# Twelve wholes of the first q product in the lead instead of eleven, so that later q products begin and end with a turn

## The chip, the cores and the metric

The kernel runs on one core of one Trainium2 chip. The metric is the device time of one execution in microseconds (us); the median of three runs is given, and one more execution was profiled. Engines are named as in the profile: PE (matrix multiplies, with PEld its weight loads), DVE (vector), ACT (activations), POOL (general), SP (issues most DMAs).

## The reference

```python
h = _layernorm(x) * (1 + ca) + sa
x = x + ga * A(h)          # attention: H = 32 heads of 16, one shared k and v
h = _layernorm(x) * (1 + cb) + sb
x = x + gb * B(h)          # (h @ w_gate) * (h @ w_up) @ w_down
# A: q = h @ wq; k = h @ wk; v = h @ wv
#    p = softmax(q k^T / 4) over all 2048 keys; o = p v; o @ wo
# S = 2048 rows, D = 512, F = 1792; six modulation rows from silu(c) @ w_mod
```

## The kernel before

The 2048 rows are cut into 4 blocks of 512 queries. A *unit* `u` is 4 heads of one block, so there are 32 units, and each runs over 16 key tiles of 128 keys. One key tile of one unit is a *turn*; `attend(u, kt)` writes out two turns. In a turn PE makes four score matmuls (`sc`, L621, `qk_exp`), ACT takes the exponential of each (`P`, L623), and PE multiplies the exponentials of the turn before with v (`pv`, L632, eight instructions into one held bank). Beside that runs a pass that finds the row maxima of a later unit: four matmuls (`mx`, L570) per turn, each reduced by DVE (`mpart`, L574).

Score and max matmuls contract over 50 and 48 rows, so two of them fit in the array at once, in the upper and the lower 64 rows. Projections are fed into the same stream as `Group`s. A q product (`q_proj`, one 128-column part of one query block) is a `Group` of 12 steps. In attention each step is cut into two halves of 64 rows (`half(r)`, L492), which stand in the halves of the array that scores and maxima leave free; before attention a step is one full matmul (`whole()`, L501). All steps of a group add up in one PSUM bank named `side` (L485). There are 16 q products of which the first is not in the queue `qs`; the queue holds 15.

The order inside a turn is written out by hand. While a q product is under way it is

```python
FEW = "e1 m0 e0 x1 m0 x1 e0 x1 m0 x1 e1 m0"    # e score, m max, x half of a product
```

and the odd turn of a pair swaps the halves 0 and 1. So a turn has four places `x` for one half of the array, a pair has eight, and a q product fills three pairs. If a product ends at a place, `side_half` begins the next one in the queue at the following place of the same turn. When no product is left, the order is `NO_SIDE`, without `x`. Later, in the feed-forward stage, it is `MANY`.

When a product has all its halves, it is put in `ended`; after the twelve places of the turn `finish` is called: ACT copies the bank to SBUF (`qf`, L514), POOL splits the copy into two 16-bit parts (L515, L516), SP stores them to DRAM (L518), from where `load_q` (L535) reads them for the max pass of a later unit.

The eight PSUM banks go round in a queue. `ps_mx` and `ps_sc` take the oldest bank and put it at the queue's end at once, so that the next matmul that is given that bank waits for its reader (DVE for `mx`, ACT for `sc`). `ps_hold` takes the oldest bank out of the queue until `ps_give`. During attention one bank is held for `pv`, one for `side`, and one for a short time by the transposition of the maxima (`mxt`, L598, once per unit) and by the sums of the late weights (L916). After the last key tile of a unit ACT copies the `pv` bank out (`ev`, L638).

The first half of a product in a turn also waits for an exponential of the turn before when the product changes its half of the array (L496). A product that begins does not change.

Before attention there are 30 steps of a *lead* (`for n in range(LEAD)`, L1103), which does the first maxima and other preparation. In its last four steps it also emits wholes of `qs[0]`, as many as `Q_BURSTS` says. What is left of `qs[0]` goes to attention.

Of the kernel before, what the change touches and what calls it, by code (L numbers as in the profile page):

```python
# [35 lines left out]
NHF = 12  # L36
M_STEP = 23
PAIRED = 14
Q_BURSTS = {26: 3, 27: 3, 28: 3, 29: 2}

CHANNEL = {0: KC - 1, 3: 0, 4: 1, 6: 2}
LOW = -3.0e38
# [12 lines left out]
def adaln_mqa_glu_kernel(ctx: ExitStack, tc: tile.TileContext, x_in, wq_in, wk_in, wv_in, wo_in,  # L55
# [1047 lines left out]
    for n in range(LEAD):  # L1103
# [6 lines left out]
        if n in first:  # L1110
            first[n]()
        for _ in range(Q_BURSTS.get(n, 0)):
            qs[0].whole()
# [166 lines left out]
```

## Time and profile before

| | |
|---|---|
| median of 3 runs | 1682.76 us (1682.55 to 1683.22) |
| profiled execution | 1682.67 us, of which the span of the program is 1680.6 us |
| PE busy | 1656.3 us, 99% of the span |
| DVE busy | 1390.0 us, 83% |
| ACT busy | 1216.1 us, 72% |
| POOL busy | 518.1 us, 31% |

The busy share of PE alone says little, because matmuls are pipelined and their ends are modelled. What a turn costs is read from the timeline: the distance from a turn's first score matmul (L621) to that of the next. Attention begins at 74.38 us. Turns are counted from 0 below; turn 2 begins at 79.58 us. The q products are in turns 0 to 85.

### The profile page before, as it was taken

The numbers are of one execution on the slowest core, as the hardware profiler recorded it, in microseconds if no ns is written. First come the engines' busy times: TensorE is split into PE (matmuls) and PEld (weight loads), VectorE is DVE, ScalarE is ACT, GpSimd is POOL, SyncE is SP. The second block draws the span as 40 slices with busy tenths as digits, with TensorE's granted clock in tenths as the row PEclk, the third lists the DMA queues.
The fourth block names the chain that finished last, engine by engine and source line by source line (L and its number), as shares of the span: only waits on it lengthen the run. The fifth ranks groups of instructions, "written<-read, shape, count | busy, mean of one in ns | idle before, by whom it ended". The sixth has DMA issues, their size and how long they took to land.

```text
span 1680.6 us, 33352 instructions
## 1 busy us (share of the span) xinstructions
PE 1656.3 (99%) x12749; PEld 535.4 (32%) x12749; DVE 1390.0 (83%) x2365; ACT 1216.1 (72%) x2288; POOL 518.1 (31%) x690
## 2 busy tenths in 40 slices
PE   8999999999999999999999999999999999999999
PEld 3333333222223333333333333333333333334444
DVE  7999999999989999999989999999998999703110
ACT  5688888888787778777777777877777777772010
POOL 5745354626676740200140211101032111112230
PEclk9999999999999999999999999999999999999999
DMA  6112122211321200001100000000010000001000
GB/s 245 72 40 88 54 88 61 94 48 50 84 66 56 85 22 9 17 10 29 35 15 12 15 15 10 16 10 17 24 32 12 23 16 6 12 5 49 13 1 25
DMA packets 48556, 66.33 MB, mean 39 GB/s; under 512 B 14726, under 2 KB 29194, under 8 KB 48396
## 3 DMA queue, kind: packets, MB, share of 16 engines
q1 hardware_dynamic: 46812, 63.87, 12.2%
q8 instruction: 100, 1.64, 0.4%
q14 instruction: 60, 0.49, 0.1%
q10 hardware_dynamic: 1584, 0.33, 0.1%
HBM read 51.05 MB, written 8.65 MB: 36 GB/s over the span
## 4 chain that ended last, share of the span: by engine, by line
PE 87%; DVE 9%; ACT 2%; DMA 1%; issue 0%; ACTq 0%; DVEq 0%
PE side L485 50%; PE pv L632 27%; DVE mpart L574 8%; PE sc L621 5%; PE mx L570 3%; ACT P L623 2%; PE mx L765 1%; DMA xbig<-in_A_x_dram 1%; PE mxt L598 0%; DVE bs L238 0%; PE sc L570 0%; PE pk L274 0%; DMA wkv<-in_A_wv_dram 0%; DVE rel L579 0%; PE part L267 0%
## 5 line engine op out<-in xcount | busy, mean ns | idle before, releaser
L574 DVE TENSOR_REDUCE mpart<-mx 128x1 f32<-128x512 f32 x2016 | 1266.1, 683 | 91.6 <-PE mx L570 88.3
L623 ACT ACTIVATE P<-sc 128x512 f32<-128x512 f32 x2048 | 1092.0, 599 | 264.6 <-PE sc L621 223.1
L621 PE MATMUL sc<-sst,kst 50*128 50x512 f16 x2048 | 661.0, 379 | 1.0 <-DVE mpart L574 0.8
L570 PE MATMUL mx<-kst,sst 48*128 48x512 f16 x2032 | 617.3, 377 | 6.5 <-DVE mpart L574 3.8
L632 PE MATMUL pv<-P,vst 128*32 128x512 f32 x4096 | 545.3, 605 | 1.2
L485 PE MATMUL side<-h2T,wg 64*128 64x512 f16 (+1 forms) x1168 | 284.3, 378 | 0.1
L485 PE MATMUL side<-h2T,wu 64*128 64x512 f16 (+1 forms) x1166 | 282.9, 378 | 0.1
L485 PE MATMUL side<-wd,glu 64*128 64x512 f16 (+1 forms) x1008 | 234.1, 378 | 0.0
L818 POOL TENSOR_SCALAR glu<-gf 128x512 f16<-128x512 f32 x56 | 34.7, 620 | 617.2 <-DVE gf L817 538.9
L621 PEld LDWEIGHTS <-kst 50*128 50x128 f16 x2048 | 175.2, 94 | 129.4 <-issue 109.6
L570 PEld LDWEIGHTS <-sst 48*128 48x128 f16 x2064 | 183.9, 94 | 58.7 <-issue 37.4
L485 PEld LDWEIGHTS <-wg 64*128 64x128 f16 (+1 forms) x1168 | 100.9, 94 | 202.7 <-ACT P L623 95.0
L485 PEld LDWEIGHTS <-wu 64*128 64x128 f16 (+1 forms) x1166 | 100.8, 95 | 200.2 <-ACT P L623 92.5
L632 PEld LDWEIGHTS pv<-P,vst 128*32 128x32 f32 x4096 | 80.8, 108 | 218.8 <-issue 202.8
L485 PEld LDWEIGHTS <-glu 64*128 64x128 f16 (+1 forms) x1008 | 89.1, 95 | 163.2 <-ACT P L623 63.0
L817 DVE TENSOR_TENSOR gf<-side,g 128x512 f32<-128x512 f32 x56 | 38.3, 684 | 115.8 <-PE side L485 82.5
L485 PE MATMUL side<-h,wq 64*128 64x512 f16 (+1 forms) x349 | 92.5, 376 | 0.0
L812 ACT ACTIVATE g<-side 128x512 f32<-128x512 f32 x56 | 33.2, 593 | 81.5 <-PE side L485 81.5
L485 PE MATMUL side<-wo,och 64*128 64x512 f16 (+1 forms) x336 | 79.3, 378 | 0.0
L819 POOL TENSOR_TENSOR glu<-gf,glu 128x512 f16<-128x512 f32 x56 | 65.0, 1161 | 4.7
L200 POOL TENSOR_SCALAR rv<-st 128x1 f32<-128x1 f32 (+1 forms) x20 | 4.6, 228 | 158.3 <-DVE st L725 143.2
L666 POOL TENSOR_TENSOR oc<-oc,rr 128x512 f32<-128x512 f32 x15 | 19.1, 1275 | 107.4 <-DMA sst<-qd 94.3
(223 smaller groups left out, 810.5 us busy)
## 6 DMA issues: line engine op xcount, KB each, us to landing
wsl<-in_B_w_gate_dram SPq DMA_DIRECT2D x32, 224.0 KB
wsl<-in_B_w_up_dram SPq DMA_DIRECT2D x32, 224.0 KB
wsl<-in_B_w_down_dram SPq DMA_DIRECT2D x28, 256.0 KB
sst<-qd SPq DMA_DIRECT2D x180, 32.0 KB
oc<-ev SPq DMA_DIRECT2D x128, 32.0 KB
rr<-ri SPq DMA_DIRECT2D x16, 256.0 KB
xl<-in_A_x_dram SPq DMA_DIRECT2D x16, 256.0 KB
qd<-q SPq DMA_DIRECT2D x15, 256.0 KB
```

The lines of the kernel that those rows point to most:

```text
L485: return nc.tensor.matmul(self.p, left[64 * r0:64 * r1], right[64 * r0:64 * r1], start=start, stop=self.ended())
L570: nc.tensor.matmul(m, s[64 * a:64 * a + 48, p, t * 128:(t + 1) * 128], w[64 * a:64 * a + 48, :], start=(i == 0), stop=(i == len(keys) - 1))
L574: nc.vector.tensor_reduce(part, m, axis=AX.X, op=OP.max)
L621: nc.tensor.matmul(t, kst[64 * a:64 * a + 50, kt * 128:(kt + 1) * 128], s[64 * a:64 * a + 50, p, :], start=True, stop=True)
L623: ex = nc.scalar.activation(ptl[u, kt, p, a], t, AF.Exp)
L632: nc.tensor.matmul(pvb[u][32 * j:32 * j + 32, :], vst[:, kt, :], ptl[u, kt, p, a], start=(kt == 0), stop=(kt == KT - 1))
L666: eng.tensor_tensor(o, o, st["r"], op=OP.mult)
L765: nc.tensor.transpose(st["p"][:, t * 128:(t + 1) * 128], n2s[b, t][:, k * 128:(k + 1) * 128], ident)
L812: nc.scalar.activation(st["g", f], p, AF.Copy, scale=2.0 ** -45)
L817: nc.vector.tensor_tensor(gf, p, st["g", f], op=OP.mult)
L818: nc.gpsimd.tensor_scalar(st["glu"][:, 0, f, :], gf, 1.0, 0.0, op0=OP.mult, op1=OP.add)
L819: nc.gpsimd.tensor_tensor(st["glu"][:, 1, f, :], gf, st["glu"][:, 0, f, :], op=OP.subtract)
```

## The change

The lead emits three wholes of `qs[0]` in its last step instead of two, so that all twelve steps of that product are done, and its `finish`, before attention begins.

```diff
-Q_BURSTS = {26: 3, 27: 3, 28: 3, 29: 2}
+Q_BURSTS = {26: 3, 27: 3, 28: 3, 29: 3}
```

Before, one whole (two halves) of `qs[0]` was left: its first half took one place of turn 0, the other three places of that turn stayed empty, its last half took the first place of turn 1, and the next product took the three places behind it. From there each product began with three halves in an odd turn and ended with one half six turns later. Thirteen turns (7, 13, ..., 79) held the end of one product and the beginning of the next. Now the next product begins at the first place of turn 0, and each one fills six turns: it ends with the last place of turns 5, 11, 17, ..., and the next opens turns 6, 12, 18, ..., 78. The last product ends in turn 83 instead of 85, so turns 84 and 85 are written in the order without places for products. The PE's order and waits from turn 87 on are the same in both kernels.

The order on ACT from the last step of the lead (`modT` is part of the lead's preparation) to the end of the first unit, before:

```order
L195 ACTIVATE modT_177<-mx 128x4x32
L623 ACTIVATE P<-sc 128x512 x8
L514 ACTIVATE qf<-side,qvs 128x512
L623 ACTIVATE P<-sc 128x512 x24
L514 ACTIVATE qf<-side,qvs 128x512
L623 ACTIVATE P<-sc 128x512 x24
L514 ACTIVATE qf<-side,qvs 128x512
L603 ACTIVATE mt_1555<-mxt 16x128
L623 ACTIVATE P<-sc 128x512 x16
L638 ACTIVATE ev<-pv,evs 128x512
L623 ACTIVATE P<-sc 128x512 x8
L514 ACTIVATE qf<-side,qvs 128x512
```

And the same stretch of ACT now:

```order
L195 ACTIVATE modT_177<-mx 128x4x32
L514 ACTIVATE qf<-side,qvs 128x512
L623 ACTIVATE P<-sc 128x512 x24
L514 ACTIVATE qf<-side,qvs 128x512
L623 ACTIVATE P<-sc 128x512 x24
L514 ACTIVATE qf<-side,qvs 128x512
L623 ACTIVATE P<-sc 128x512 x8
L603 ACTIVATE mt_1559<-mxt 16x128
L623 ACTIVATE P<-sc 128x512 x16
L514 ACTIVATE qf<-side,qvs 128x512
L638 ACTIVATE ev<-pv,evs 128x512
L623 ACTIVATE P<-sc 128x512 x24
```

Every copy `qf` stands two turns (eight exponentials) earlier, the first of them ahead of attention; one of them now stands right ahead of the copy `ev` of a unit's end, as another does at the end of the fourth unit, while before the two met once, at the end of the third.

The second half of turn 7 on PE before, where `side_1273` is the bank of the product that begins in this turn (its first half stands just ahead of these rows), `mx_1270` took its bank ahead of them, and the bracket names the engine whose work a matmul waits for:

```order
L621 LDWEIGHTS kst_130
L621 MATMUL sc_1276<-sst0_126,kst_130 128x512 [waits DVE_49]
L485 LDWEIGHTS wq_110
L485 MATMUL side_1273<-h16_178,wq_110 128x512
L570 LDWEIGHTS sst1_127
L570 MATMUL mx_1280<-kst_130,sst1_127 128x512 [waits Activation_49]
L485 LDWEIGHTS wq_110
L485 MATMUL side_1273<-h16_178,wq_110 128x512
L621 LDWEIGHTS kst_130
L621 MATMUL sc_1285<-sst0_126,kst_130 128x512 [waits DVE_49]
L570 LDWEIGHTS sst1_127
L570 MATMUL mx_1288<-kst_130,sst1_127 128x512 [waits Activation_49]
```

The second half of turn 6 on PE now, the first turn that a product opens after another has ended, with `side_1242` its bank:

```order
L621 LDWEIGHTS kst_130
L621 MATMUL sc_1249<-sst0_126,kst_130 128x512 [waits DVE_49]
L485 LDWEIGHTS wq_110
L485 MATMUL side_1242<-h16_178,wq_110 128x512
L570 LDWEIGHTS sst1_127
L570 MATMUL mx_1253<-kst_130,sst1_127 128x512 [waits Activation_49]
L485 LDWEIGHTS wq_110
L485 MATMUL side_1242<-h16_178,wq_110 128x512
L621 LDWEIGHTS kst_130
L621 MATMUL sc_1258<-sst0_126,kst_130 128x512 [waits Activation_49]
L570 LDWEIGHTS sst1_127
L570 MATMUL mx_1261<-kst_130,sst1_127 128x512 [waits DVE_49]
```

Before, two product banks were out of the queue in the second half of such a turn, so the last two max matmuls were given banks that exponentials of the same turn were still to read. Now the ended product's bank is back in the queue before the next product takes one: the third max matmul is given that bank and waits for `qf`, and the last one waits for a DVE reduction, as in a turn within a product.

## The prediction

> **What bounds the kernel now.** I read the page first, then the busy time by windows for the stretch in which the q products run, then the timeline of single turns. Columns of the first row: engine, busy us, instructions; of the window row: length, then busy us (and count) of PE, PEld, DVE, ACT, POOL, the granted clock, DMA share and GB/s; of the timeline: start, duration, engine, line, what.
>
> ```profile
> PE 1656.3 (99%) x12749; PEld 535.4 (32%) x12749; DVE 1390.0 (83%) x2365; ACT 1216.1 (72%) x2288; POOL 518.1 (31%) x690
> 150.00:200.00 50.00, 49.92 (x414) 16.04 (x414) 48.49 (x84) 42.05 (x82) 22.46 (x23) 1.00 0.19 60
> ```
>
> In this stage PE and DVE are both nearly full, ACT has about a sixth of its time free, and the clock is full. Neither PE nor DVE is the limit by itself; a ring of the two is. Turn 6 (89.6 to 92.1) shows it; it lies within a product (first max matmul and its reduction, third and fourth max, `pv`, and the first score of turn 7, which comes together with its first max):
>
> ```profile
> 89.60 0.39 PE L570 MATMUL mx<-kst,sst 48*128 48x512 f16 x1
> 90.05 0.69 DVE L574 TENSOR_REDUCE mpart<-mx 128x1 f32<-128x512 f32 x1
> 90.48 0.38 PE L570 MATMUL mx<-kst,sst 48*128 48x512 f16 x1
> 90.80 0.37 PE L570 MATMUL mx<-kst,sst 48*128 48x512 f16 x1
> 91.10 1.06 PE L632 MATMUL pv<-P,vst 128*32 128x512 f32 x8
> 92.10 0.39 PE L621 MATMUL sc<-sst,kst 50*128 50x512 f16 x1
> ```
>
> The first max matmul starts at 89.60, its reduction runs from 90.05 to 90.74, the fourth max matmul, which is given the same bank, starts at 90.80, `pv` follows 0.30 later, and the next turn 1.00 after that: 2.50 us. Now turn 7, in which one product ends and the next begins (third and fourth max, `pv`, and the first scores of turns 8 and 9, with the ACT and DVE rows between):
>
> ```profile
> 92.52 2.06 ACT L623 ACTIVATE P<-sc 128x512 f32<-128x512 f32 x4 [0.44 <-PE mx L570]
> 93.17 0.37 PE L570 MATMUL mx<-kst,sst 48*128 48x512 f16 x1
> 93.66 0.37 PE L570 MATMUL mx<-kst,sst 48*128 48x512 f16 x1
> 93.96 1.06 PE L632 MATMUL pv<-P,vst 128*32 128x512 f32 x8
> 94.45 0.71 ACT L514 ACTIVATE qf<-side,qvs 128x512 f32<-128x512 f32 x1
> 94.96 0.39 PE L621 MATMUL sc<-sst,kst 50*128 50x512 f16 x1
> 95.41 3.19 DVE L574 TENSOR_REDUCE mpart<-mx 128x1 f32<-128x512 f32 x5 [0.38 <-PE mx L570]
> 97.46 0.39 PE L621 MATMUL sc<-sst,kst 50*128 50x512 f16 x1
> ```
>
> It takes 94.96 - 92.10 = 2.86 us. Four exponentials in 2.06 us, the last one about 0.6, have a pitch of about 0.49, so the first ends at 93.12 and the second at 93.61: exactly 0.05 ahead of the third max matmul (93.17) and the fourth (93.66), which wait for them, since with a second product bank held they were given banks of this turn's scores. DVE then stands still for 0.38 us. So such a turn costs 2.86 - 2.50 = 0.36 us, on the path that sets the pace, and turn 8 (2.50) gives none of it back. That the second bank does it and not the end of a product is shown by turn 85, which has a product's end and no beginning, and takes 299.31 - 296.81 = 2.50:
>
> ```profile
> 294.31 0.39 PE L621 MATMUL sc<-sst,kst 50*128 50x512 f16 x1
> 296.81 0.39 PE L621 MATMUL sc<-sst,kst 50*128 50x512 f16 x1
> 299.31 0.39 PE L621 MATMUL sc<-sst,kst 50*128 50x512 f16 x2
> 304.08 0.39 PE L621 MATMUL sc<-sst,kst 50*128 50x512 f16 x2
> 306.46 0.39 PE L621 MATMUL sc<-sst,kst 50*128 50x512 f16 x2
> ```
>
> **The change, part by part.** *Removed: thirteen mixed turns.* Turns 7, 13, ..., 79 no longer hold two product banks: 13 x 0.36 = 4.68 us less. I take the price of turn 7 for all; those with the weights' sums may give a little more.
>
> *Shorter: turns 84 and 85.* They lose their product places. With such places a turn took 2.50 (294.31 to 296.81), without them 306.46 - 304.08 = 2.38: 2 x 0.12 = 0.24 less.
>
> *Added: the copy `qf` ahead of the exponentials of an opening turn.* It is the same copy as before, but it no longer has the 0.36 of the mixed turn to hide in. Queued behind it on ACT are the four exponentials of the opening turn, for whose first the fourth score matmul waits, and behind that the fourth max. The nearest row is the copy `ev`, equally long, ahead of the exponentials of turn 18, in a turn without a mixed one ahead of it:
>
> ```profile
> 119.12 0.39 PE L621 MATMUL sc<-sst,kst 50*128 50x512 f16 x1
> 121.47 0.71 ACT L638 ACTIVATE ev<-pv,evs 128x512 f32<-128x512 f32 x1
> 121.68 0.39 PE L621 MATMUL sc<-sst,kst 50*128 50x512 f16 x1
> 124.18 0.39 PE L621 MATMUL sc<-sst,kst 50*128 50x512 f16 x1
> ```
>
> Turn 18 takes 124.18 - 121.68 = 2.50: the copy fits in the 0.44 that ACT idles in a plain turn (the row at 92.52), and costs nothing. The third max matmul is to wait for `qf` itself; it would start 2.35 after the start of the turn ahead (as 94.45 - 92.10), end at 3.07, which is 0.57 in the opening turn, and that matmul comes at about 0.88 in a turn (90.48 - 89.60). So I take 0 for the nine opening turns that have nothing else on ACT (6, 12, 24, 36, 42, 48, 54, 60, 72). Bounds: no gain is possible, since the ring from the first max to the fourth stays; at most the whole 0.71 delays ACT instead of the 0.57 after which the next instruction starts in the rows below, 0.14 each, 1.3 in all.
>
> The Trainium skill ("ScalarE: Activation LUTs", section "What ACT_TABLE_LOAD costs") speaks against this a little: by it a copy of 512 columns with one pointer operand takes 186 + 93 + 0.833 x 512 = 706 ns and back-to-back activations overlap by 93 ns, so `qf` would hold ACT for 0.61 us. By that figure each of the nine turns would cost about 0.04, and the gain would be 0.4 us smaller. The trace's 0.71 agrees with the duration; for the overlap it shows more, 0.71 - 0.57 = 0.14.
>
> *Moved: two openings meet a unit's end.* `qf` and `ev` now stand together ahead of turns 18 and 66; before, they met once, ahead of turn 50:
>
> ```profile
> 204.91 0.71 ACT L514 ACTIVATE qf<-side,qvs 128x512 f32<-128x512 f32 x1
> 205.48 0.72 ACT L638 ACTIVATE ev<-pv,evs 128x512 f32<-128x512 f32 x1
> 205.42 0.39 PE L621 MATMUL sc<-sst,kst 50*128 50x512 f16 x1
> 206.05 2.10 ACT L623 ACTIVATE P<-sc 128x512 f32<-128x512 f32 x4
> 206.74 0.37 PE L621 MATMUL sc<-sst,kst 50*128 50x512 f16 x1
> 208.06 0.39 PE L621 MATMUL sc<-sst,kst 50*128 50x512 f16 x1
> ```
>
> Each copy holds ACT 0.57 (204.91 to 205.48 to 206.05). The exponentials start 0.63 in the turn, the fourth score matmul waits for the first of them until 1.32, and the turn ends 1.32 later: 2.64. Now the turn ahead is not 2.86 but 2.56 (turn 17: 121.68 - 119.12, in which `pv` waits for a new bank), so the exponentials start at 2.35 + 0.57 + 0.57 - 2.56 = 0.93, the first ends near 1.57, the score starts at 1.63, and the turn takes 1.63 + 1.32 = 2.95 instead of 2.50. Two such: +0.90. Turn 50 falls to 2.50 (-0.14), and turn 49 keeps 0.06 of `pv`'s wait (+0.06). Bounds for each meeting: 0.14, as in turn 50, and 0.57, a whole copy.
>
> *Moved: two openings meet the transposition of the maxima*, turns 30 and 78. Where `qf` and that step met before:
>
> ```profile
> 235.89 0.71 ACT L514 ACTIVATE qf<-side,qvs 128x512 f32<-128x512 f32 x1
> 236.40 0.28 PE L598 MATMUL mxt<-ident,mm 128*16 128x128 f32 x1
> 236.71 0.27 ACT L603 ACTIVATE mt<-mxt 16x128 f16<-16x128 f32 x1
> ```
>
> There `qf` began 0.51 ahead of the turn and `mt` started at 0.31. Now `qf` begins 0.15 ahead of it (2.50 - 2.35), `mt` starts at 0.57 - 0.15 = 0.42, and DVE's part of it with the reductions behind it 0.11 later: 2 x 0.11 = 0.22 more, between nothing and 0.36 each, all the cover that the mixed turn gave.
>
> *Moved: the twelfth whole and the first `qf` into the lead.* DVE has work there without a gap from 71.51 to 95.04:
>
> ```profile
> 71.51 23.53 DVE L574 TENSOR_REDUCE mpart<-mx 128x1 f32<-128x512 f32 x38 [0.39 <-PE mx L570]
> 72.49 0.82 PE L485 MATMUL side<-h,wq 128*128 128x512 f16 x3
> 73.85 0.60 PE L485 MATMUL side<-h,wq 128*128 128x512 f16 x2
> 74.81 4.18 ACT L623 ACTIVATE P<-sc 128x512 f32<-128x512 f32 x8 [0.63 <-PE mx L570]
> ```
>
> So the third whole (0.82 - 0.60 = 0.22) and the exponentials, which now begin behind `qf`, about 0.5 after 74.81, are covered as long as the eight max matmuls of turns 0 and 1 arrive in time; following their banks by hand, I estimate that each has about 0.3 or more to spare. Without this cover it costs up to 0.5. With it, turn 2 can begin up to 0.1 earlier, since turn 1 was mixed too; I take -0.10. POOL's and SP's shares of `qf` move forward with it; POOL is 31% busy, and they stay behind no work that PE waits for.
>
> *Sum:* -4.68 - 0.24 + 0.90 - 0.14 + 0.06 + 0.22 - 0.10 = -3.98, against the profiled execution's 1682.67 us: 1678.7. That execution lies 0.09 below the median, so the same holds for that. From turn 87 on the program is unchanged and each part starts on other parts' ends or counted turns, so the whole is kept to the end.
>
> **The rivals.** (1) *Openings pay in part.* The exponentials come late in each opening turn: the 1.3 of the bound, 2 x (0.57 - 0.45) = 0.24 more at the meetings, 2 x (0.36 - 0.11) = 0.50 at the transpositions. Gain 3.98 - 2.04 = 1.9, time 1680.7. For it: `qf` is now in a turn without spare time; against it: turn 18. (2) *The time is given back later.* If late weights or their POOL work set the start of the feed-forward stage, the 4 us become a wait there: 1682.7. Against it: POOL's longest waits are for DVE, in the feed-forward stage itself (total us, times, longest), so POOL has time to spare there:
>
> ```profile
> POOL glu L818 <- DVE gf L817: 538.9, 53, 29.2
> ```
>
> (3) *Slower: each opening turn becomes like a meeting.* If the exponentials of all thirteen opening turns begin at 0.93 instead of 0.43, each turn takes 0.45 more: 13 x 0.45 = 5.85, against 4.68 + 0.24 + 0.08 + 0.10 = 5.10 that goes: +0.75, 1683.4. It decides from 5.10 / 13 = 0.39 per opening, for which ACT would have to be held by `qf` about 1.1 us; the `ev` rows show 0.57. (4) *The mixed turn's cost stays*, because it comes from the end of a product and not from the second bank: then nothing goes but 0.24, and the meetings cost 0.9: 1683.4 too. Turn 85 speaks against it.
>
> **How the numbers follow.** Forecast 0.70, rival 1 0.12, rival 2 0.08, rivals 3 and 4 0.06 together, more than 4.8 gained 0.04. The predicted time is that of the forecast, 1678.7. The bounds of its own terms, taken the good way (meetings 0.14 each, transpositions nothing), give 4.8, or 1677.8; some more in the mixed turns with sums gives 1677.5. Upwards the range takes in rival 1 and a part of what lies behind it: 1681.0. About 0.2%, or 3.4 us, is what a measurement of this kernel can tell from no change. The forecast lies 0.6 beyond it, and its dear bounds inside; of its 0.70 I give 0.65 to faster by more than that, with 0.03 of the good tail: 0.68. Rivals 1 and 2 and most of 3 and 4 are within: 0.28. Slower by more: 0.04.
>
> **What would show it.** Right: turns 7, 19, 25 and so on take 2.50; turns 6, 24, 36 take 2.50 with `qf` ahead of their exponentials; DVE has no idle of 0.38 at a product's beginning; turns 18 and 66 take about 2.95; turn 86 begins about 4.0 earlier than before, and the end as well. Wrong: opening turns of 2.6 or more everywhere (rival 1 or 3), a later wait of PE that grew by what was saved (rival 2), or the last two max matmuls of some turn in six still waiting for exponentials (rival 4).

## The result, and the profile after

The changed kernel takes 1679.41 us (median of 14 runs), the kernel before 1683.27 us beside it: a ratio of 0.9978, 95% interval 0.9971 to 0.9985. The forecast was 1678.7 us, faster by more than can be told from no change. The profiled execution takes 1679.23 us, 3.44 less than that of before; its span is 1677.1. A turn is counted from its first score matmul to that of the next.

The page's engine row and the window that was shown of before (length, then busy us and count of PE, PEld, DVE, ACT, POOL, granted clock, DMA share, GB/s), now of the changed kernel:

```profile
PE 1652.6 (99%) x12748; PEld 535.7 (32%) x12748; DVE 1389.8 (83%) x2365; ACT 1214.6 (72%) x2288; POOL 518.0 (31%) x690
150.00:200.00 50.00, 49.57 (x418) 16.12 (x415) 49.08 (x86) 42.55 (x84) 24.45 (x26) 1.00 0.19 56
```

DVE is busier in the same 50 us (49.08 instead of 48.49) because it no longer stands still once in six turns; PE is 0.35 less busy, which is a new wait, shown below. The timeline of the changed kernel around turns 6 and 7 (the first score of turns 6, 7 and 8, third and fourth max of turn 6, the ACT rows of turns 5 and 6, and DVE):

```profile
87.55 2.06 ACT L623 ACTIVATE P<-sc 128x512 f32<-128x512 f32 x4 [0.44 <-PE mx L570]
88.79 8.79 DVE L574 TENSOR_REDUCE mpart<-mx 128x1 f32<-128x512 f32 x14
89.47 0.71 ACT L514 ACTIVATE qf<-side,qvs 128x512 f32<-128x512 f32 x1
89.63 0.39 PE L621 MATMUL sc<-sst,kst 50*128 50x512 f16 x1
90.05 2.09 ACT L623 ACTIVATE P<-sc 128x512 f32<-128x512 f32 x4
90.52 0.38 PE L570 MATMUL mx<-kst,sst 48*128 48x512 f16 x1
90.83 0.37 PE L570 MATMUL mx<-kst,sst 48*128 48x512 f16 x1
92.13 0.39 PE L621 MATMUL sc<-sst,kst 50*128 50x512 f16 x1
94.63 0.39 PE L621 MATMUL sc<-sst,kst 50*128 50x512 f16 x1
```

Turn 7 takes 94.63 - 92.13 = 2.50 instead of 2.86. Turn 6, which a product now opens, takes 2.50 as well: `qf` sits in ACT's idle time, the exponentials start 0.42 in the turn, the third max comes at 0.89 with `qf`'s bank free by then, and the fourth at 1.20. DVE's fourteen reductions run without a gap. Where an opening meets a unit's end it is otherwise (turns 17 and 18; the fourth score of turn 18 is the row at 122.56):

```profile
118.38 0.39 PE L621 MATMUL sc<-sst,kst 50*128 50x512 f16 x1
120.73 0.71 ACT L514 ACTIVATE qf<-side,qvs 128x512 f32<-128x512 f32 x1
121.30 0.72 ACT L638 ACTIVATE ev<-pv,evs 128x512 f32<-128x512 f32 x1
120.94 0.39 PE L621 MATMUL sc<-sst,kst 50*128 50x512 f16 x1
121.87 2.10 ACT L623 ACTIVATE P<-sc 128x512 f32<-128x512 f32 x4
122.56 0.37 PE L621 MATMUL sc<-sst,kst 50*128 50x512 f16 x1
123.88 0.39 PE L621 MATMUL sc<-sst,kst 50*128 50x512 f16 x1
```

The exponentials start 0.93 in the turn, the fourth score at 1.62, and the turn takes 2.94 instead of 2.50. Turn 66 takes the same. And one turn became slower that the prediction expected to become shorter, turn 31. Its rows, with those of turn 30 that lead to it (PE's `mxt` stands ahead of the first score of turn 30; the scores at 154.34 and 157.34 open turns 31 and 32):

```profile
151.41 0.28 PE L598 MATMUL mxt<-ident,mm 128*16 128x128 f32 x1
152.11 0.28 DVE L604 SCALAR_TENSOR_TENSOR mt<-mxt,mt 16x128 f16<-16x128 f32 x1
152.76 1.16 POOL L516 TENSOR_TENSOR q<-qf,q 128x512 f16<-128x512 f32 x1
153.95 0.33 SPq L518 DMA_DIRECT2D qd<-q  x1
154.32 0.42 SPq L897 DMA_DIRECT2D wsl<-in_B_w_gate_dram  x1
154.84 1.23 SPq L608 DMA_DIRECT2D sst<-mt  x2
154.34 0.39 PE L621 MATMUL sc<-sst,kst 50*128 50x512 f16 x1
157.34 0.37 PE L621 MATMUL sc<-sst,kst 50*128 50x512 f16 x1 [0.43 <-DMA sst<-mt]
```

Before, the two DMAs that bring the maxima to the next unit's scores were issued 0.61 after that `mxt` (152.42):

```profile
153.03 1.22 SPq L608 DMA_DIRECT2D sst<-mt  x2
```

Now they are issued 3.43 after it (154.84 - 151.41), although `mt` is ready at 152.39 (152.11 + 0.28): on SP they stand behind the product's store `qd`, which waits until 153.92 for POOL's second split (152.76 + 1.16), and behind a weight load. The first score of the next unit waits for them, and turn 31 takes 3.00.

The distance between the first scores of turns 2 and 87 holds all places of q products but those of turns 0 and 1. It is free of the lead, which ends at other times in other executions (turn 2 begins between 78.95 and 80.93 us in the profiles of this study), and so it is compared below, in us. Each ratio is to runs of the kernel before that were made beside that kernel (medians 1683.27, 1683.03 and 1683.00).

| kernel | turn 2 to turn 87 | median of all runs | ratio to before, 95% interval |
|---|---|---|---|
| before | 222.13 | 1683.27 | |
| changed | 218.55 | 1679.41 | 0.9978 (0.9971 to 0.9985) |
| no begin where another ends | 218.82 | 1679.20 | 0.9978 (0.9969 to 0.9987) |
| store half a turn later | 218.08 | 1678.88 | 0.9976 (0.9967 to 0.9985) |
| lead alone | 222.35 | 1683.30 | 1.0001 (0.9992 to 1.0010) |
| further bank held | 223.08 | 1684.51 | 1.0006 (0.9997 to 1.0015) |
| changed, again | 218.51 | 1679.31 | 0.9979 (0.9970 to 0.9988) |
| turn 0 left empty | 217.74 | 1678.64 | 0.9974 (0.9964 to 0.9985) |
| turn 6 left empty | 217.47 | 1678.91 | 0.9977 (0.9968 to 0.9986) |

### The profile page after: what moved, and what is told of

Read it like the earlier page. It is cut to its first block, busy times and chain, and to the rows that moved or that the text cites. A ratio compares the mean times of both kernels' runs of the same rounds, so it can differ in the third digit from the quotient of the medians.

```text
span 1677.1 us, 33341 instructions
## 1 busy us (share of the span) xinstructions
PE 1652.6 (99%) x12748; PEld 535.7 (32%) x12748; DVE 1389.8 (83%) x2365; ACT 1214.6 (72%) x2288; POOL 518.0 (31%) x690
## 4 chain that ended last, share of the span: by engine, by line
PE 88%; DVE 9%; ACT 1%; DMA 1%; issue 0%; ACTq 0%; SPq 0%; DVEq 0%
PE side L485 51%; PE pv L632 27%; DVE mpart L574 8%; PE sc L621 5%; PE mx L570 3%; ACT P L623 1%; PE mx L765 1%; DMA xbig<-in_A_x_dram 0%; PE mxt L598 0%; PE sc L570 0%; DVE bs L238 0%; DMA wkv<-in_A_wv_dram 0%; PE pk L274 0%; PE part L267 0%; DVE rel L579 0%
```

## The experiments

The theory: a turn that ends one product and begins another holds two product banks, the ring of banks for scores and maxima is one shorter, and the last two max matmuls wait for exponentials of their own turn. Rivals: the lead's whole brings the gain, or a product's end or beginning costs by itself.

**No begin where another ends.** The lead stays as before; products may not share a turn.

```diff
 # side_half, lead and Q_BURSTS as before
             if not cur:
+                if ended and ended[0] in qs:
+                    return
                 if cur is not second and second and second[0].turn != now[0]:
```

> The lead as before (eleven wholes); a product may not begin in a turn in which another ended, so turn 1 keeps only the last half of the first product and the next products open turns 2, 8, 14, ..., 80. Theory (the price is that of two product banks out of the queue at once): turns 7, 13, ..., 79 fall from 2.86 to 2.50 although the lead is untouched; the one meeting of qf and ev (turn 50) costs 2.95 instead of 2.64, the transpositions in turns 14 and 62 0.1 each; together about -4.2 us against before, 0.5 less time than the changed kernel. Rival (the gain comes from the first product being done in the lead): no change from before.

Turns 7, 19, 25 and so on fall to 2.50, and turn 8, which a product now opens, keeps its 2.50 (first scores of turns 7, 8 and 9):

```profile
93.70 0.39 PE L621 MATMUL sc<-sst,kst 50*128 50x512 f16 x1
96.21 0.39 PE L621 MATMUL sc<-sst,kst 50*128 50x512 f16 x1
98.71 0.39 PE L621 MATMUL sc<-sst,kst 50*128 50x512 f16 x1
```

All thirteen mixed turns are gone without the lead's whole. Turn 50 takes 2.94 as expected, turns 14 and 62 0.12 and 0.09 more. What was not expected is turn 2, at 3.37 instead of 2.50; without its 0.87 the stretch would be 217.95, 4.18 less than before, as the -4.2 says. TensorE ran at half clock there, which is taken up at the end. So the lead is not what brings the gain.

**The lead alone.** Twelve wholes in the lead, and the old phase of the products behind it.

```diff
 # the changed kernel
+    skipped = [5]
+
     def side_half(r, cur=cur):
+        if skipped[0]:
+            skipped[0] -= 1
+            return
```

> Twelve wholes in the lead as in the changed kernel, but the first five product places of attention are left empty, so that the next product begins at the second place of turn 1 and the thirteen mixed turns stand as before. Theory (the lead's whole is worth nothing by itself): the time of before within 0.3 us, turns 7, 13, ..., 79 at 2.86. Rival (the lead's whole brings the gain): about -3.9 us.

No turn from 3 to 86 differs from before by more than 0.03, turn 7 is 2.86 again, and the ratio is 1.0001:

```profile
93.64 0.39 PE L621 MATMUL sc<-sst,kst 50*128 50x512 f16 x1
96.50 0.39 PE L621 MATMUL sc<-sst,kst 50*128 50x512 f16 x1
```

Only turn 2 is longer, 2.69; turns 0 and 1, which hold two product halves less than before, are shorter by 0.11 and 0.40. The whole in the lead gains nothing by itself that these runs could show; it moves the phase of the products.

**A further bank held.** Within a product, where nothing ends or begins, a bank is taken out of the queue from the second product place on.

```diff
 # the changed kernel, attend
                 a = a if style is NO_SIDE else a ^ turn
+                t_ = u * KT + kt + turn
+                if style is FEW and j == 5 and t_ % 6 == 3 and 9 <= t_ <= 81:
+                    spare.append(ps_hold("mx"))
...
             assert not sync["due"]
+            while spare:
+                ps_give(spare.pop())
```

> The changed kernel, with one further PSUM bank taken out of the queue from the second product place to the end of the turn in thirteen turns that lie within a product (9, 15, ..., 81); nothing is computed in it. Theory (the second bank is the price, whatever is in it): the thirteen turns rise by 0.36 each, those with sums or a transposition by somewhat more or less, +4.7 us against the changed kernel, so about 0.8 slower than before. Rival (the price is that of a product's end or of the first half of another): the time of the changed kernel.

Turn 9 (its first score, third score, third and fourth max, the first score of turn 10, and ACT and DVE):

```profile
97.94 0.39 PE L621 MATMUL sc<-sst,kst 50*128 50x512 f16 x1
98.37 2.07 ACT L623 ACTIVATE P<-sc 128x512 f32<-128x512 f32 x4 [0.44 <-PE mx L570]
98.61 0.38 PE L621 MATMUL sc<-sst,kst 50*128 50x512 f16 x1
99.02 0.37 PE L570 MATMUL mx<-kst,sst 48*128 48x512 f16 x1
99.50 0.37 PE L570 MATMUL mx<-kst,sst 48*128 48x512 f16 x1
100.80 0.39 PE L621 MATMUL sc<-sst,kst 50*128 50x512 f16 x1
101.26 3.19 DVE L574 TENSOR_REDUCE mpart<-mx 128x1 f32<-128x512 f32 x5 [0.38 <-PE mx L570]
```

It takes 2.86, with the third max 1.08 and the fourth 1.56 after the turn's first score and DVE idle for 0.38: a copy of the mixed turn of before (1.07, 1.56 and 0.38), without an end or a beginning. The stretch grows by 223.08 - 218.55 = 4.53 against 4.7 expected. The price is that of the bank. The stretch is 0.95 longer than that of before; the medians do not show this by themselves, since the interval of their ratio includes 1.

**The store half a turn later.** This tests why turn 31 takes 3.00.

```diff
 # the changed kernel, q_proj
-            nc.sync.dma_start(d, q16)
+            after(1, lambda: nc.sync.dma_start(d, q16))
             qd[b, ch] = d
```

> The changed kernel, with the store of a finished product's 16-bit halves issued half a turn later on SP, so that the store of the maxima (mt) in turn 30 stands ahead of it. Theory (turn 31 takes 3.00 because mt's DMA stands on SP behind the product's store, which waits for POOL): turn 31 falls to 2.50 and everything else stays, -0.5 us against the changed kernel, about -4.3 against before. Rival (turn 31 is long because of the exponentials that qf delayed in turn 30): turn 31 stays at 3.00.

SP's rows of turn 30 and the first scores of turns 31 and 32:

```profile
152.50 1.23 SPq L608 DMA_DIRECT2D sst<-mt  x2
154.34 0.33 SPq L518 DMA_DIRECT2D qd<-q  x1
154.74 0.39 PE L621 MATMUL sc<-sst,kst 50*128 50x512 f16 x1
157.24 0.39 PE L621 MATMUL sc<-sst,kst 50*128 50x512 f16 x1
```

Turn 31 takes 2.50, and it is the only turn from 0 to 86 that differs by more than 0.01. Turn 30, with its exponentials behind `qf`, takes 2.72 with this edit and without, so SP's order is the cause. The gain of 0.47 shows in the stretch alone; the medians are too close.

**Products that open odd turns.** The copies `ev` stand ahead of turns 18, 34, 50 and 66, and the transpositions ahead of the first scores of turns 14, 30, 46, 62 and 78. All of these are even, so products that open odd turns should meet neither. Such a phase is made in two ways, and the changed kernel is run once more beside them.

```diff
 # the changed kernel: turn 0 left empty
+    skipped = [4]
+
     def side_half(r, cur=cur):
+        if skipped[0]:
+            skipped[0] -= 1
+            return
```

```diff
 # the changed kernel: turn 6 left empty
     def side_half(r, cur=cur):
+        if now[0] == 12:
+            return
```

> The changed kernel once more, beside the next two. Expected: turns 18 and 66 at 2.94, turn 31 at 3.00, about 3.8 us less than before; the start of attention may move by some tenths with the lead.

> The changed kernel with the four product places of turn 0 left empty, so that each product opens an odd turn (1, 7, 13, ...), where no unit ends and no maxima are transposed. Theory (a meeting of qf and ev costs 0.44, one of qf and the transposition 0.1, and a product's store ahead of that of the maxima 0.5): turns 18 and 66 fall to 2.50, 30 to 2.84, 31 to 2.50, 78 to 2.93, while 84 and 85 take 2.50 again; -1.3 us against the changed kernel. Rival (an opening in an odd turn costs as much, in other places): the time of the changed kernel. Turns 0 to 2 may grow, since PE has less to do in turn 0; where such a turn was empty before, the granted clock fell to half for 3.4 us and turn 2 took 3.37.

> The changed kernel with the product places of turn 6 left empty instead, so that products open the odd turns 7, 13, and so on, and turns 0 to 5 stay as they are. Theory: turns 18, 30, 31, 66 and 78 fall as in the kernel with turn 0 empty, 84 and 85 rise by 0.1 each, turn 6 takes 2.50 or less, and the start keeps its clock: -1.3 us against the changed kernel, -5 against before. Rival (an opening in an odd turn costs as much): the time of the changed kernel.

The repeated kernel has the same turns (18 and 66 at 2.94, 31 at 2.96). With an odd phase turns 18, 31 and 66 fall to 2.50, as expected. Turns 30 and 78 fall from 2.72 to 2.63 and from 2.76 to 2.69 or 2.70. The expectation counted these two from `mxt`, which stands ahead of the first score, and so named 2.84 and 2.93; the falls, 0.09 and 0.07, are those that it named. ACT's and PE's rows around turn 18 with turn 6 left empty show why (PE's are the first scores of turns 18 and 19):

```profile
121.43 0.71 ACT L638 ACTIVATE ev<-pv,evs 128x512 f32<-128x512 f32 x1
121.64 0.39 PE L621 MATMUL sc<-sst,kst 50*128 50x512 f16 x1
122.12 2.06 ACT L623 ACTIVATE P<-sc 128x512 f32<-128x512 f32 x4
124.05 0.71 ACT L514 ACTIVATE qf<-side,qvs 128x512 f32<-128x512 f32 x1
124.14 0.39 PE L621 MATMUL sc<-sst,kst 50*128 50x512 f16 x1
124.62 2.10 ACT L623 ACTIVATE P<-sc 128x512 f32<-128x512 f32 x4
```

The two copies stand one turn apart, and each finds its own idle time. Not expected were turn 80, 0.24 longer in this kernel (0.23 with turn 0 empty), and turn 49, 0.09 longer. In turn 80 the exponentials start 0.78 after the first score (279.98 to 280.76) instead of 0.48; why, stays open, and so does turn 49. The stretch falls by 1.08 with turn 6 empty and by 0.81 with turn 0 empty (whose turn 2 takes 2.69), against 1.3 expected. Both beat the kernel before clearly. Against the changed kernel only the stretch shows the gain: the medians beside it, 1678.64 and 1678.91 against 1679.31, differ by less than its own runs do among themselves (1678.92 to 1680.18).

## Why the prediction was right, and where it was not

The medians fell by 3.86, against 3.98 forecast. By its interval the ratio allows 2.5 to 4.9, so that nearness proves little; the terms are judged by the turns.

*Mixed turns, 13 x 0.36:* right, and shown by three kernels: this one, the one without mixed turns, and the one with the held bank. In the changed kernel nine of them fell by 0.36, turns 13 and 79 by 0.42, turn 49 by 0.30 (it keeps the 0.06 of `pv`'s wait). Turn 31 did not, for the reason below; in the kernel without mixed turns it fell by 0.35, and the thirteen by 4.7 together.

*Turns 84 and 85, 0.24:* 0.11 and 0.13, and 0.03 in turn 86.

*Openings at no cost:* right. All nine take what they took before, within 0.01. The rule of the Trainium skill ("ScalarE: Activation LUTs", section "What ACT_TABLE_LOAD costs") gave an estimate of 0.04 each. The trace does not bear that cost out: `qf` let the next activation start after at most 0.58 (89.47 to 90.05), not 0.61, and that start, 0.42 in the turn, is no later than in turn 7 of before, where no copy precedes it (92.52 - 92.10). Rival 1 is refuted by the same nine turns.

*Meetings with a unit's end, 0.45 each:* 0.44 in both, and gone in the odd phase. Turn 50 fell by 0.14 as written.

*Meetings with the transposition, 0.11 each:* 0.09 and 0.07 for turns 30 and 78 themselves.

*The step that failed* is the sentence that POOL's and SP's shares of `qf` "stay behind no work that PE waits for". It looked at what `qf`'s followers stand behind, and not at what stands behind them. In turn 30 the DMA of the maxima stands behind the store, and the first score of the next unit waited 0.43 for it: turn 31 was to fall by 0.36 and rose by 0.14, which is 0.50 of the sum. In turn 78 the same order cost nothing visible. There the DMA was issued at 277.70; by the 2.50 from its issue to that score in the other case (154.84 to 157.34), an estimate, the maxima were in place at 280.20, 0.51 ahead of the first score of turn 80 (280.71), since turns 78 and 79 are longer.

*The lead, -0.10:* not settled. Turn 2 began at 79.61 instead of 79.58. Turns 0 and 1 together took 5.04 instead of 5.20, in all five profiles in which they have the changed kernel's places, so 0.16 was gained there, although PE stood still for 0.39 in turn 1, until a half of the product could start at 77.44 behind an exponential. DVE's row had no gap, as foreseen. Whether the third whole, 0.22 of PE's time, made attention start later can't be told: in the seven profiles with the same lead it starts between 74.22 and 76.25.

*Kept to the end:* right. The shift is -3.54 at turn 87 and -3.67 at the last turn, so rival 2 is out. Rival 3 is out with the nine openings, rival 4 with the turns that fell to 2.50 and with the held bank.

Together -3.58 from turn 2 to 87, where the terms without the lead gave -3.88; the difference is the 0.50 of turn 31 less 0.2 by which other terms were better than written.

## What to carry to other kernels

Where buffers go round in a queue, an accumulator that begins before another has been read out shortens the ring for everyone else (here 0.36 us for each turn of 2.50); read the price from a turn that has only one of the two, and prefer a phase in which they don't overlap. When a step moves, follow each of its instructions to its queue and ask what stands behind it there, not only what it waits for; here a store that waited for POOL held up the short DMA behind it by 2.4 us. Look where small copies meet: here one copy of 0.71 us in ACT's idle stretch cost nothing, and two that met cost 0.44.

## What the runs showed of the hardware that was not expected

In the profiled execution of the first experiment, where turns 0 and 1 hold only two product halves, the clock of TensorE fell to half. Windows just before, during and after, and the first scores of turns 2 and 3:

```profile
75.00:79.00 4.00, 3.57 (x22) 1.21 (x22) 4.00 (x8) 3.82 (x8) 0.00 (x0) 0.99 0.63 193
79.00:82.30 3.30, 3.30 (x18) 0.74 (x12) 2.56 (x5) 1.86 (x4) 2.35 (x3) 0.50 0.00 0
80.32 0.60 PE L621 MATMUL sc<-sst,kst 50*128 50x512 f16 x1
83.69 0.39 PE L621 MATMUL sc<-sst,kst 50*128 50x512 f16 x1
```

PE counts as busy for 3.57 of the 4.00 us ahead of it, and yet matmuls then take 0.60 instead of 0.39 and turn 2 takes 3.37, 0.87 more. The trace has the half clock from 78.91 to 82.32, for 3.41 us. The Trainium skill ("TensorE: Matmul & The Clock Gate", section "Part 1: The HAM clock gate (the "warmup" mystery)") says that the clock halves after an idle window of about 3.4 us that runs freely. The length of the slow stretch agrees, but PE was not idle ahead of it. That it was thinly used is not shown to be the reason: from 75 to 79 us the kernel before has 21 matmuls and 3.79 us busy, the changed kernel 26 and 3.61, against 22 and 3.57 here, and both kept their clock. What set it off stays open.

The first experiment does not lose this time in every execution. In five of its ten runs the mean granted clock is 0.998, which allows at most 8.4 us at half clock; every profile of this study has 6.8 us at half clock ahead of attention, and that leaves no room for another 3.4. The kernel with turn 0 alone empty kept its clock in its profiled execution.
